# A planner's waiting times behind transfers, and the queue that stores projected values

## The chip, the cores and the metric

The kernel runs on one core of a Trainium2 chip. The metric is the time on the device in microseconds (us). Before the change it is 1178.59 us, the median of three runs (1177.14 to 1179.32).

## The reference

Four layers run in turn on one sequence of 2048 tokens with 640 channels: a sliding-window attention, a channel MLP, and both again with the same weights. Each adds to the residual `x`.

```python
# A: layernorm, then attention with W=8 keys at distance 2, 32 heads of 20 channels
qkv = x @ wqkv                                   # 640 -> 1920
idx = pos[:, None] - arange(8)[None, :] * 2      # each token looks at 8 earlier ones, two apart
attn = softmax(where(idx >= 0, q . k[idx] * 20**-0.5, -1e9))
x = x + (attn . v[idx]).reshape(S, 640) @ wo
# B: layernorm twice (once outside, once inside), then
x = x + gelu(y @ w1 + b1) @ w2 + b2              # 640 -> 1536 -> 640
# A, B, A, B
```

All arrays are float32.

## The kernel before, in words

**Tiles.** Tokens are split by parity (the window steps by two) and then into halves. That makes four units of 512 tokens, each 4 tiles of 128. With two layers of attention there are eight unit steps, numbered 0 to 7 (4 to 7 are the second layer). A unit's attention is done in four groups of eight heads, so there are 32 groups. The MLP of a unit walks through 12 blocks of 128 hidden channels; unit 0's MLP is done in two halves of 256 tokens.

**Precision.** Every float32 operand of a product is split into two fp16 parts, high and low, and three of the four partial products are taken. The split costs ScalarE (ACT) one copy and VectorE (DVE) one subtraction for each operand.

**One unit's way.** Layernorm (ACT, L524 to L560) gives `y`. It is split (L566 on ACT, L568 on DVE) and turned by four DMA transposes that SyncE's queue issues (L570). TensorE (PE) multiplies it by `wqkv`, 15 matmuls for each token tile and head group (L602). ACT copies each result from PSUM to `ev` (L617). Two token tiles of one head group make one `ev` buffer, of which there are three, and a DMA that ACT issues stores it to memory in `spill` (L623, called a put here; 64 of them). SyncE's queue fetches it back with a halo of neighbouring tokens into the single `qk` and the single `v` buffer (L642). DVE does the attention of a group there: products with q (L684), sums (L688), softmax (L693 to L703), products with v (L710), sums over the window (L718, L722). The result is split again (L729, L732) and turned by four DMA transposes (L745); PE multiplies it by `wo` (L756), and DVE adds the product to `x` (L762). A second layernorm and a third set of transposes follow (L570 again), and then the MLP: L810 is the first product, L816 the gelu, L819 and L821 its split, L831 the second product into five PSUM accumulators, L866 the addition to `x`. The MLP's weights are split once (L425, L426), stored by ACT's queue as `mw`, and loaded again for every unit by SyncE's queue (L803), into three buffers for each of the two matrices. The first product of the MLP waits for the split of all weights.

**What sets the order.** Nothing is scheduled by hand. Each step is handed to the class `Plan` as an operation: its engine, an estimated duration, a priority, what it needs, what it gives, and the buffers that it uses. `Plan.run` plays them in its own clock: of the operations that are ready it takes the earliest, and of equals the one with the lower priority. Then the instructions are emitted in the order of the planned start times, so each engine's queue has a fixed order. On the chip an engine that reaches an instruction early waits for it, and everything behind it on that engine waits too. So the planner's estimates set only the order.

**A transfer in the plan.** When an operation with `move` is placed, it joins its queue `REACH` later (L243), is drained there packet by packet (`SHARE` makes packets slower while two queues are busy), and counts as landed `LAND` later (L164). An operation that needs it may start `LAG["sp"]`, 0.05, after that (L182). A transpose occupies SyncE's queue for 1.45 in the plan (L378).

Of the kernel before, what the change touches and what calls it, by code (L numbers as in the profile page):

```python
# [20 lines left out]
GC = D // NG  # L21
# [43 lines left out]
class Plan:  # L65
# [9 lines left out]


    AHEAD = 3.0
    REACH = 0.45
    LAND = 1.4

    SHARE = 1.15

    LETS = ("pv", "hlo", "lo", "at", "xb")

# [24 lines left out]
    def run(self):  # L109
# [16 lines left out]
        soon, queues, late = [], {}, []  # L126
        seen = 0.0

        def done(o, end, lag):
            for u in o["use"]:  # L130
                self.users[u] -= 1
                self.last[u] = max(self.last.get(u, 0.0), end + lag * (u[0] != "pr" or o["eng"] != "dve"))
                if not self.users[u]:
                    self.free[u[0]].append((self.last[u], self.slot[u]))
            for k in o["give"]:
                when[k] = (o["eng"], end, bool(o["move"]))
                for w in waiting.pop(k, ()):
                    left[w["n"]] -= 1
                    if not left[w["n"]]:
                        ready.setdefault(w["eng"], []).append(w)  # L140
# [14 lines left out]
        def advance(t):  # L155
            h = heads()
            if h:
                turns = (t - seen) / turn()
                for x in h:
                    x[0] -= turns  # L160
            for x in h:
                if x[0] < 1e-9:
                    queues[x[2]["eng"]].pop(0)
                    late.append((t + self.LAND, x[2]))  # L164
            for b, o in [v for v in soon if v[0] <= t]:
                soon.remove((b, o))
                queues.setdefault(o["eng"], []).append([*o["move"], o])
            for e, o in [v for v in late if v[0] <= t]:
                late.remove((e, o))
                done(o, e, self.LAG["sp"])  # L170
            return t

        def start(o):
            t = clock[o["eng"]]
            if o["lazy"]:
                t = max(t, seen - self.AHEAD + sum(x[0] * x[1] for q in queues.values() for x in q)
                        + sum(v["move"][0] * v["move"][1] for _, v in soon))
            if o["pair"] and o["eng"] == "dve":
                t = max(t, port)
            for k in o["need"]:  # L180
                e, w, moved = when[k]
                w = w + (self.LAG["sp"] if moved else self.LAG[e] if e != o["eng"] else 0.06 * (e != "pe"))  # L182
                t = max(t, w)
            if o["pair"] and o["eng"] == "pool":
                for i, (a, b) in enumerate(reversed(shut)):
                    if t >= b:
                        break
                    if a <= t:
                        t = b + 0.1 * (i == 0)
                        break  # L190
            new = {}
            for u in o["use"]:
                if u in self.slot:
                    t = max(t, self.since[u])
                else:
                    fs = self.free[u[0]]
                    if u[0] in self.ORDERED and self.line[u[0]][self.turn.get(u[0], 0)] != u:
                        return None
                    i = new.get(u[0], 0)
                    if i >= len(fs):  # L200
                        return None
                    t = max(t, sorted(fs)[i][0])
                    new[u[0]] = i + 1
            return t

        total = len(self.ops)
        while len(order) < total:
            best = None
            for e, ops in ready.items():
                pick = None  # L210
                for o in ops:
                    t = start(o)
                    if t is None:
                        continue
                    key = (max(t - o["wait"], clock[e] + 0.05), o["prio"], o["n"])
                    if pick is None or key < pick[0]:
                        pick = (key, t, o)
                if pick and (best is None or (pick[1], pick[0]) < (best[1], best[0])):
                    best = pick
            then = event()  # L220
            if best is None and then == math.inf:
                raise RuntimeError(f"the plan is stuck: {[u for u in self.slot if self.users[u]]}")
            if best is None or then <= best[1]:
                seen = advance(then)
                continue
            _, t, o = best
            e = o["eng"]
            ready[e].remove(o)
            d = o["dur"]
            if o["table"] and o["table"] != table:  # L230
                table = o["table"]
                d += self.SWITCH
            for u in o["use"]:
                if u not in self.slot:
                    fs = self.free[u[0]]
                    fs.sort()
                    self.turn[u[0]] = self.turn.get(u[0], 0) + 1
                    self.since[u], self.slot[u] = fs.pop(0)
            o["at"] = t
            order.append(o)  # L240
            clock[e] = t + d
            if o["move"]:
                soon.append((t + self.REACH + 0.2 * (o["dur"] > 1), o))  # L243
                continue
            if e == "dve":
                kind = o["give"][0][0]
                if o["pair"]:
                    if shut and t - shut[-1][1] < 0.05 and before != "pv" and kind not in self.LETS:
                        shut[-1][1] = t + d
                    else:  # L250
                        shut.append([t, t + d])
                before = kind
            elif e == "pool" and o["pair"] and d > 1:
                port = t + d
            done(o, t + d, self.LAG[e])
# [6 lines left out]
def packet_time(n):  # L262
    return 0.0075 + n / 26.9e3
# [11 lines left out]
def sliding_dilated_then_mlp_kernel(  # L275
# [99 lines left out]
        plan.add(by, 0.1 if by == "act" else 0.38, prio, emit, need, give, use, move=(kb * 1e3 / 16 / packet, packet_time(packet)), lazy=lazy)  # L375

    def dma_transpose(prio, emit, need=(), give=(), use=()):
        plan.add("sp", 1.45, prio, emit, need, give, use, move=(80, packet_time(256) + 0.0045))  # L378

    def mm(cols, n, prio, emit, need=(), give=(), use=()):  # L380
        plan.add("pe", cols / 2400.0 + 0.0028 * n, prio, emit, need, give, use)
# [203 lines left out]
    def qkv(n):  # L585
# [6 lines left out]
        for k, (g, b) in enumerate(halves):  # L592
# [27 lines left out]

            def put(g=g, b=b, ek=ek):
                to = spill[la][par]
                nc.scalar.dma_start(  # L623
                    bass.AP(tensor=to.tensor, offset=to.offset + (g * 3 * ROWS + HALO + start + 2 * b) * GC,
                            ap=[[M * GC, P], [ROWS * GC, 3], [1, 2 * GC]]),
                    tile_of(*ek).rearrange("p a t c -> p a (t c)"))

            dma(P * 6 * GC * 4 / 1e3, -310 + n, put, need=[("ev", n, 2 * b + i, g) for i in range(2)],
                give=[("put", n, g, b)], use=[ek], by="act", packet=8 * GC)

    def fetch(G):
        n, g = divmod(G, NG)
# [319 lines left out]
```

## Time and profile before

| | |
|---|---|
| median of the runs | 1178.59 us (1177.14 to 1179.32) |
| the profiled execution's own time | 1177.89 us |
| its span, from the first instruction to the last | 1176.0 us |
| TensorE's granted clock over the span | 0.998 of full speed |
| busy: PE, DVE, ACT, POOL | 1157.5, 991.6, 511.5, 150.9 us |

The span is 1.9 us shorter than the execution's time. Busy time is the time in which an engine had at least one instruction in work. In rows of instructions the columns are start and duration in us, engine, line, operation, output<-input, shapes and count, and in square brackets the idle time of the engine just before and what ended it. `SPq` and `ACTq` are DMA issues on SyncE's and ACT's queue. In rows of waits the columns are who waited for whom, the sum in us, how often, and the longest.

### The profile page before, as it was taken

What the parts mean: (1) busy time and instruction counts of PE and PEld (TensorE: products, weight loads), DVE (VectorE), ACT (ScalarE), POOL (GpSimd) and SP (SyncE); (2) the same over time, 40 slices, a digit from 0 to 9 for tenths busy, and PEclk for the clock granted to TensorE, in tenths of its full rate; (3) what the DMA queues carried; (4) which work ended last, traced back from release to release, by engine and by line L of the source; (5) the groups of instructions that cost most, each with busy time, mean ns of one, the idle gap of its engine ahead of it and who ended that gap; (6) DMA issues with size and microseconds to landing.
All of it is one profiled execution on the core that took longest, in us unless ns stands there. A gap on an engine that the chain in (4) does not pass through costs nothing.

```text
span 1176.0 us, 17291 instructions
## 1 busy us (share of the span) xinstructions
PE 1157.5 (98%) x6902; PEld 626.5 (53%) x6902; DVE 991.6 (84%) x939; ACT 511.5 (43%) x925; POOL 150.9 (13%) x96
## 2 busy tenths in 40 slices
PE   8999999999999999999999999999999999999998
PEld 5444445577554455545554555555456555555554
DVE  7899999999899999999999999999999996311211
ACT  5485334436445345732537352376235423512121
POOL 1020102023011201320221012002120100000000
PEclk9999999999999999999999999999999999999999
DMA  9999997787776477567755865576555845633432
GB/s 294 300 329 283 373 349 195 212 269 243 210 205 196 162 215 188 176 191 190 193 180 177 212 167 188 202 166 186 188 177 161 246 158 128 154 103 102 145 101 79
DMA packets 219773, 235.01 MB, mean 200 GB/s; under 512 B 129884, under 2 KB 170412, under 8 KB 219692
## 3 DMA queue, kind: packets, MB, share of 16 engines
q1 hardware_dynamic: 190636, 194.57, 56.7%
q10 hardware_dynamic: 29056, 39.33, 9.6%
q8 instruction: 54, 0.88, 0.3%
q14 instruction: 27, 0.22, 0.1%
HBM read 158.93 MB, written 44.78 MB: 173 GB/s over the span
## 4 chain that ended last, share of the span: by engine, by line
PE 55%; DVE 28%; DMA 6%; issue 6%; ACT 4%; SPq 1%; POOL 0%; ACTq 0%; DVEq 0%; POOLq 0%
PE ps L602 20%; PE acc L831 14%; PE ps L810 14%; PE ps L756 7%; DVE pr L684 6%; DVE pr L710 6%; DVE pr L718 4%; DVE sm L688 4%; DMA yT<-w 2%; DVE act L821 1%; DMA qk<-spill 1%; ACT junk L528 1%; DMA act<-in_B_w_dram 1%; DVE w L722 1%; ACT junk L524 1%
## 5 line engine op out<-in xcount | busy, mean ns | idle before, releaser
L602 PE MATMUL ps<-wq,yT 128*128 128x480 f16 x1920 | 393.0, 367 | 4.8 <-DMA yT<-w 3.6
L831 PE MATMUL acc<-c,act 128*128 128x512 f16 (+1 forms) x2310 | 331.3, 299 | 1.1 <-DVE act L821 0.6
L810 PE MATMUL ps<-yT,c 128*128 128x512 f16 (+1 forms) x1620 | 328.6, 355 | 0.8 <-DMA c<-mw 0.8
L602 PEld LDWEIGHTS <-yT 128*128 128x128 f16 x1920 | 187.7, 98 | 207.0 <-DMA yT<-w 5.1
L831 PEld LDWEIGHTS <-act 128*128 128x128 f16 x2310 | 181.7, 98 | 143.3 <-DVE act L821 1.2
L810 PEld LDWEIGHTS <-c 128*128 128x128 f16 x1620 | 154.5, 98 | 147.1 <-DMA c<-mw 1.2
L816 ACT ACTIVATE act<-ps,b 128x512 f32<-128x512 f32 (+1 forms) x108 | 68.7, 637 | 272.4 <-PE ps L810 268.0
L684 DVE TENSOR_TENSOR pr<-qk 128x2560 f32<-128x2560 f32 x64 | 181.5, 2836 | 4.1 <-DMA qk<-spill 4.1
L710 DVE TENSOR_TENSOR pr<-sm,v 128x2560 f32<-128x2560 f32 x64 | 179.7, 2819 | 0.2
L688 DVE TENSOR_REDUCE sm<-pr 128x128 f32<-128x2560 f32 x64 | 179.5, 2805 | 0.1
L821 DVE TENSOR_TENSOR act<-act 128x512 f16<-128x512 f32 (+1 forms) x108 | 72.3, 671 | 124.1 <-ACT act L819 123.8
L718 DVE TENSOR_TENSOR pr<-pr 128x1280 f32<-128x1280 f32 (+1 forms) x128 | 144.8, 1151 | 0.2
L756 PE MATMUL ps<-wo,yT 128*128 128x320 f16 x960 | 132.4, 299 | 5.9 <-DMA yT<-ohl 3.3
L617 ACT ACTIVATE ev<-ps 128x480 f32<-128x480 f32 x128 | 71.6, 563 | 148.8 <-PE ps L602 137.3
L756 PEld LDWEIGHTS <-yT 128*128 128x128 f16 x960 | 93.7, 98 | 44.4 <-DMA yT<-ohl 4.3
L732 POOL TENSOR_TENSOR ohl<-w,ohl 128x640 f16<-128x640 f32 x24 | 67.1, 2796 | 379.2 <-ACT ohl L729 379.2
L541 POOL TENSOR_TENSOR ln<-ln,half 128x2 f32<-128x2 f32 (+1 forms) x30 | 36.2, 1207 | 451.0 <-ACT ln L538 451.0
L524 ACT ACTIVATE junk<-xf 128x640 f16<-128x640 f32 x56 | 41.1, 734 | 79.2 <-DVE xf L762 60.3
L819 ACT ACTIVATE act<-act 128x512 f16<-128x512 f32 (+1 forms) x108 | 62.4, 580 | 2.6
L568 DVE TENSOR_TENSOR w<-w,w 128x640 f16<-128x640 f32 x60 | 51.2, 874 | 1.5 <-ACT w L566 1.5
L560 ACT ACTIVATE w<-xf,ln 128x640 f32<-128x640 f32 x56 | 49.7, 908 | 1.9 <-DVE w L568 1.6
L566 ACT ACTIVATE w<-w 128x640 f16<-128x640 f32 x60 | 42.7, 727 | 12.5 <-DVE w L568 7.2
(53 smaller groups left out, 515.1 us busy)
## 6 DMA issues: line engine op xcount, KB each, us to landing
c<-mw SPq DMA_DIRECT2D x216, 320.0 KB, 3.2
spill<-ev ACTq DMA_DIRECT2D x64, 480.0 KB, 4.3
qk<-spill SPq DMA_DIRECT2D x32, 880.0 KB, 5.5
v<-spill SPq DMA_DIRECT2D x32, 880.0 KB, 4.5
qk<-spill SPq DMA_DIRECT2D x32, 320.0 KB, 3.2
act<-in_B_w_dram SPq DMA_DIRECT2D x24, 320.0 KB, 5.9
mw<-c ACTq DMA_DIRECT2D x24, 320.0 KB, 5.8
xf<-in_A_x_dram SPq DMA_DIRECT2D x16, 320.0 KB, 6.3
```

The lines of the kernel that those rows point to most:

```text
L602: nc.tensor.matmul(ps, transposed(yk)[:, a * KD + k, t * P:(t + 1) * P], wq[:, b, k, g], start=first and j == 0, stop=last and j == len(to ...
L617: act(3 * GC, -400 + n, lambda i=i, pk=pk, ek=ek: nc.scalar.activation(tile_of(*ek)[:, :, i], tile_of(*pk)[:, :3 * GC].rearrange("p (a c) ...
L684: nc.vector.tensor_mul(tile_of(*pk), w[:, HALO + m + t0:HALO + m + t0 + EH, None, :].to_broadcast([P, EH, W, GC]), windows(w, t0, [GC, W], ...
L688: dve(E, G - 0.7, lambda pk=pk, t0=t0: nc.vector.tensor_reduce(lg(t0, t0 + EH).rearrange("p t w h -> p (t w h)"), tile_of(*pk).rearrange(" ...
L710: nc.vector.tensor_mul(tile_of(*vk).rearrange("p t w (h d) -> p t (w h) d", d=DH), lg(t0, t0 + EH).rearrange("p t w h -> p t (w h)")[:, :, ...
L718: dve(EH * w * GC, G - 0.9, lambda vk=vk, w=w: nc.vector.tensor_add(tile_of(*vk)[:, :, 0:w], tile_of(*vk)[:, :, 0:w], tile_of(*vk)[:, :, w ...
L732: eng.tensor_sub(tile_of(*hk)[:, :, 1, g * GC:(g + 1) * GC], ot(), hi())
L756: nc.tensor.matmul(tile_of(*pk)[:, :D // 2], transposed(yk)[:, a * KD + k, t * P:(t + 1) * P], wo[:, b, k, c * D // 2:(c + 1) * D // 2], s ...
L810: nc.tensor.matmul(tile_of(*pk)[:, :nt], tile_of(*ck)[:, a, k * P:(k + 1) * P], transposed(yk)[:, c * KD + k, t0 * P:t1 * P], start=i == 0 ...
L816: act(nt, -430, lambda pk=pk, h32=h32, e=e: nc.scalar.activation(tile_of(*h32)[:, :nt], tile_of(*pk)[:, :nt], AF.Gelu_apprx_tanh, bias=b1[ ...
L821: dve(nt, -1000, lambda h32=h32, hk=hk: nc.vector.tensor_sub(tile_of(*hk)[:, 1, :nt], tile_of(*h32)[:, :nt], tile_of(*hk)[:, 0, :nt]), nee ...
L831: nc.tensor.matmul(accs[k][:, c0:c0 + n], tile_of(*hk)[:, a, (i - t0) * P:(i - t0 + 1) * P], tile_of(*wk)[:, c, w0:w0 + n], start=first, s ...
```

## The change

In the plan a transfer now joins its queue 0.75 after it is placed, or after its own duration where that is longer, pays 0.2 more at the head of the queue, and lands 0.9 later (0.5 for a transpose). Who needs the data waits a further time that depends on the engine: 2.0 for TensorE, 0.7 for ACT, DVE and POOL, none for SyncE. A transfer gives its buffers back 0.7 after it lands instead of 0.05. A transpose occupies the queue for 1.75. `SHARE` goes from 1.15 to 1.08. The puts are issued by SyncE's queue instead of ACT's, and so are planned on it. No operation is added or taken away.

```diff
     AHEAD = 3.0
-    REACH = 0.45
-    LAND = 1.4
-
-    SHARE = 1.15
+    REACH = 0.75
+    LAND = 0.9
+    RAMP = 0.2
+
+    SPARE = {"pe": 2.0, "act": 0.7, "dve": 0.7, "pool": 0.7, "sp": 0.0}
+
+    SHARE = 1.08
...
-                    late.append((t + self.LAND, x[2]))
+                    late.append((t + self.LAND - 0.4 * (x[2]["dur"] > 1), x[2]))
...
-                queues.setdefault(o["eng"], []).append([*o["move"], o])
+                queues.setdefault(o["eng"], []).append([o["move"][0] + self.RAMP / o["move"][1], o["move"][1], o])
...
-                done(o, e, self.LAG["sp"])
+                done(o, e, 0.7)
...
-                w = w + (self.LAG["sp"] if moved else self.LAG[e] if e != o["eng"] else 0.06 * (e != "pe"))
+                w = w + (self.LAG["sp"] + self.SPARE[o["eng"]] if moved else self.LAG[e] if e != o["eng"] else 0.06 * (e != "pe"))
...
-                soon.append((t + self.REACH + 0.2 * (o["dur"] > 1), o))
+                soon.append((t + max(self.REACH, o["dur"]), o))
...
     def dma_transpose(prio, emit, need=(), give=(), use=()):
-        plan.add("sp", 1.45, prio, emit, need, give, use, move=(80, packet_time(256) + 0.0045))
+        plan.add("sp", 1.75, prio, emit, need, give, use, move=(80, packet_time(256) + 0.0045))
...
             def put(g=g, b=b, ek=ek):
                 to = spill[la][par]
-                nc.scalar.dma_start(
+                nc.sync.dma_start(
...
-                give=[("put", n, g, b)], use=[ek], by="act", packet=8 * GC)
+                give=[("put", n, g, b)], use=[ek], packet=8 * GC)
```

Every engine's order changes. Three places follow; line numbers after the change are three higher in this part of the kernel.

**PE, where unit 5's attention result meets `wo`.** L756 (L759 after) is the product with `wo`, L831 (L834) the MLP's second product, L810 (L813) its first. Before:

```order
L831 MATMUL acc_100<-c_83,act 128x512
L831 LDWEIGHTS act
L831 MATMUL acc_101<-c_83,act 128x128
L756 LDWEIGHTS yT_72
L756 MATMUL ps_95<-wo,yT_72 128x320
```

After:

```order
L834 MATMUL acc_100<-c_83,act 128x512
L834 LDWEIGHTS act
L834 MATMUL acc_101<-c_83,act 128x128
L813 LDWEIGHTS c_80
L813 MATMUL ps_95<-yT_73,c_80 128x512
...
L759 LDWEIGHTS yT_72
L759 MATMUL ps_96<-wo,yT_72 128x320
```

The first product of one more hidden block, 15 matmuls of 512 columns, now stands ahead of the product with `wo`. The same count for the other places where PE takes up transposed data, as the number of matmuls by which the step comes later in PE's order (minus: earlier): `wo` of units 0 to 7: -30, +18, 0, +18, +18, +15, 0, +21; `wqkv` of unit 4's first half -27 and of its second half -62, of units 5, 6 and 7 +33, +18 and +15; unit 1's MLP +24.

**DVE, where unit 4's first layernorm result is split for its transposes.** L568 (L571) is that split, L710 (L713) the products with v of group 7, L718 and L722 (L721, L725) their sums, L821 (L824) the gelu's split. Before:

```order
L710 TENSOR_TENSOR pr_77<-sm_90,v_68 128x2560
L821 TENSOR_TENSOR act<-act 128x256
L718 TENSOR_TENSOR pr_77<-pr_77 128x2x640
L821 TENSOR_TENSOR act<-act 128x256
L718 TENSOR_TENSOR pr_77<-pr_77 128x2x320
L722 TENSOR_TENSOR w_84<-pr_77 128x320
L710 TENSOR_TENSOR pr_76<-sm_90,v_68 128x2560
L821 TENSOR_TENSOR act<-act 128x256
L568 TENSOR_TENSOR w_86<-w_88,w_86 128x640
```

After:

```order
L713 TENSOR_TENSOR pr_77<-sm_90,v_68 128x2560
L824 TENSOR_TENSOR act<-act 128x256
L571 TENSOR_TENSOR w_84<-w_88,w_84 128x640
L721 TENSOR_TENSOR pr_77<-pr_77 128x2x640
L824 TENSOR_TENSOR act<-act 128x256
L571 TENSOR_TENSOR w_85<-w_86,w_85 128x640
```

The split for the first transpose moves ahead of the sums of the group's first half and of the products of its second half. Elsewhere on DVE: unit 1's last split for its MLP comes six operations later (one L684, two L688 and three softmax steps are now ahead of it), unit 4's third split ten operations earlier, unit 5's first four later, unit 6's first is unmoved, and the last operation on unit 6's attention result comes one L701 later. The split of the last MLP weight block moves from DVE's 149th to its 182nd operation.

**SyncE's queue at the start.** L421 (L424) loads `x`, L414 (L417) clears the halo, L438 (L441) loads `wqkv`, L626 is the put. Before:

```order
L438 DMA pr_77<-in_A_wqkv_dram 128x5x160 x3
L438 DMA qk_67<-in_A_wqkv_dram 128x5x160 x3
L421 DMA xf<-in_A_x_dram 128x640 x4
L414 DMA spill_136<-act 7x12x160
...
L402 DMA b_104<-in_B_b_dram 128x12x1
```

After:

```order
L441 DMA qk_67<-in_A_wqkv_dram 128x5x160 x3
L626 DMA spill_135<-ev_69 128x3x320
L424 DMA xf<-in_A_x_dram 128x640 x4
L417 DMA spill_136<-act 7x12x160
...
L405 DMA b_104<-in_B_b_dram 128x12x1
L626 DMA spill_135<-ev_70 128x3x320
```

The put, which waits for a result of PE and ACT, now stands ahead of the loads of unit 1's `x`; further on, puts stand between the loads of the weights in the same way. Puts also stand directly ahead of the transposes of units 3's and 4's attention results (L748).

## The prediction

> **What bounds the kernel now.** I read the page's busy times first, then PE's waits, then the busy times by stretches, and last the timeline at each wait.
>
> ```profile
> span 1176.0 us, 17291 instructions
> PE 1157.5 (98%) x6902; PEld 626.5 (53%) x6902; DVE 991.6 (84%) x939; ACT 511.5 (43%) x925; POOL 150.9 (13%) x96
> PE 55%; DVE 28%; DMA 6%; issue 6%; ACT 4%; SPq 1%; POOL 0%; ACTq 0%; DVEq 0%; POOLq 0%
> ```
>
> PE is idle for 1176.0 - 1157.5 = 18.5 us, and the change takes no work from it: 18.5 us is the most that an order could give. The chain that ended last still runs through DVE for 28%. The stretches say why:
>
> ```profile
> 800.00:884.00 84.00, 84.00 (x458) 42.25 (x457) 83.06 (x71) 34.21 (x57) 19.10 (x9) 1.00 0.55 178
> 990.00:1176.00 186.00, 182.20 (x1135) 97.16 (x1132) 38.47 (x59) 46.82 (x80) 1.39 (x2) 1.00 0.41 117
> ```
>
> The columns after the stretch are its length and the busy time of PE, PEld, DVE, ACT and POOL, then clock, DMA share and GB/s. From 800 to 884 both PE and DVE are busy nearly all the time, and so they are before; only from 990 is PE alone. So a wait of PE that goes shortens the kernel only if DVE can hand over earlier as well. What PE waits for:
>
> ```profile
> PE ps L602 <- DMA yT<-w: 3.6, 3, 2.0
> PE ps L756 <- DMA yT<-ohl: 3.3, 2, 2.5
> PE ps L756 <- DVE xf L762: 2.6, 3, 0.9
> PE ps L810 <- DMA c<-mw: 0.8, 1, 0.8
> ```
>
> 7.7 us is spent on transfers, 6.9 of it on transposes. That is what spare time behind transfers can reach.
>
> **The change part by part.** *Unit 4's first transpose.*
>
> ```profile
> 286.83 2.82 DVE L710 TENSOR_TENSOR pr<-sm,v 128x2560 f32<-128x2560 f32 x1
> 289.64 1.80 PE L810 MATMUL ps<-yT,c 128*128 128x256 f16 x15
> 289.90 1.55 DVE L568 TENSOR_TENSOR w<-w,w 128x640 f16<-128x640 f32 x2
> 291.28 1.79 PE L831 MATMUL acc<-c,act 128*128 128x512 f16 x12
> 291.70 2.35 DVE L718 TENSOR_TENSOR pr<-pr 128x1280 f32<-128x1280 f32 x2
> 292.91 1.80 PE L810 MATMUL ps<-yT,c 128*128 128x256 f16 x15
> 296.68 3.58 PE L602 MATMUL ps<-wq,yT 128*128 128x480 f16 x10 [1.97 <-DMA yT<-w]
> 295.00:300.00 5.00, 3.32 (x10) 1.33 (x11) 4.62 (x4) 1.12 (x3) 0.00 (x0) 0.73 1.14 326
> 300.00:305.00 5.00, 5.00 (x26) 2.46 (x25) 3.46 (x4) 0.92 (x2) 0.00 (x0) 0.92 1.26 205
> 785.00:790.00 5.00, 2.56 (x19) 1.87 (x20) 2.73 (x4) 1.37 (x2) 0.00 (x0) 1.00 1.23 185
> ```
>
> The split (L568) moves ahead of one L710 (2.82), a pair of sums like L718's 2.35, and about 0.9 of smaller steps: 6.0 us earlier on DVE. PE reaches the product 27 matmuls earlier, a group of 15 and one of 12; such groups start 1.63 us apart (289.64, 291.28, 292.91), so 3.3 us. Net 2.7, more than the 1.97 waited. I expect DVE about 1.3 us late here (below) and leave 0.5 of the wait: gain 1.5. Behind this wait the clock was 0.73 and 0.92 of full for 5 us each, so (0.27 + 0.08) x 5 = 1.75 us were lost, which go with it. The wait of 2.47 us in 785 to 790 cost no clock (1.00), so this term can as well stay or appear elsewhere; it is 1.75 or nothing at each wait of about 2 us. [...]
>
> *Units 5 and 6, and unit 2's attention.* Of the 3.6 us under L602, 1.6 belong to units 5 and 6. Their products move back by 33 and 18 matmuls. At 3.24 us for 15 of the MLP's first product and 3.26 for 24 of its second (rows below) that is 3.24 + 18 x 0.136 = 5.7 and 18 x 0.136 = 2.5 us. DVE's split moves back by 4.2 (an L688 and three small steps) and 0: net 1.5 and 2.5, enough for both: gain 1.6. Unit 2's product with `wo` waits 3.3 - 2.47 = 0.8 and moves on neither engine: gain 0.4, between 0 and 0.8.
>
> *Unit 5's attention.*
>
> ```profile
> 778.03 0.80 SPq L642 DMA_DIRECT2D qk<-spill  x2
> 779.41 9.84 SPq L745 DMA_TRANSPOSE yT<-ohl  x4
> 787.44 2.75 PE L756 MATMUL ps<-wo,yT 128*128 128x320 f16 x19 [2.47 <-DMA yT<-ohl]
> 852.52 3.24 PE ps L810 x15
> 855.75 3.26 PE acc L831 x24
> ```
>
> The transposes stand behind a fetch on SyncE's queue that waits for DVE. That order stays. PE now does 15 more matmuls first, 3.24 us, against 2.47: gain 2.47. The one MLP load that PE waited for (0.8) has 12 more matmuls, 1.6 us, ahead of its user: gain 0.8. The 2.6 us of waits for L762 are no transfers: 0, at most 2.6.
>
> *New waits.*
>
> ```profile
> 334.62 6.22 SPq L570 DMA_TRANSPOSE yT<-w x2
> 347.14 3.40 PE L810 MATMUL ps<-yT,c 128*128 128x512 f16 x15
> 376.12 2.91 SPq L570 DMA_TRANSPOSE yT<-w  x2
> 379.60 5.63 PE L602 MATMUL ps<-wq,yT 128*128 128x480 f16 x27
> yT<-w SPq DMA_TRANSPOSE x60, 4.4
> ```
>
> Unit 1's MLP had its last transpose issued near 338, 9 us ahead. DVE now does six more operations before it, 9.9 us (one L684 of 2.8, two L688 of 2.8, the rest softmax), and PE 24 more matmuls, 3.3 us; that leaves about 3 where a landing takes 4.4. Unit 4's second half had 379.60 - 376.12 = 3.5 us and keeps 3.1, since PE comes 62 matmuls earlier (2 x 3.24 + 32 x 0.136 = 10.8 us) and DVE ten operations (10.4 us). Together I charge 2.5 us, between 0 and 5.
>
> *The puts.*
>
> ```profile
> L623 ACTq DMA_DIRECT2D spill<-ev x64: 366/367/1044, 20.1 to 853.2; - x64
> SPq L803 <- PE acc L831: 197.2, 84, 16.0
> ```
>
> 64 x 0.37 = 23.5 us of issuing leaves ACT (43% busy) and lands on SyncE's queue, which waits 197 us for MLP buffers alone and so has room. Behind a waiting put stand fetches, transposes and loads. No row shows a put on that queue; ahead of units 3's and 4's transposes it costs at most 480 KB at 326 GB/s, 1.5 us, covered by the 18 matmuls (2.5 us) that those products move back. I take 0.
>
> *Weights.*
>
> ```profile
> 169.30 0.82 DVE L426 SCALAR_TENSOR_TENSOR c<-act,c 128x640 f16<-128x640 f32 x1
> 225.62 5.08 PE L810 MATMUL ps<-yT,c 128*128 128x256 f16 x45
> ```
>
> 33 operations of attention, 39 us, now stand ahead of the last weight split: 170 + 39 = 209 against PE's first MLP product at 225.6. The cover is 17 us; I take 0.
>
> Sum for PE: 1.5 + 1.75 + 1.6 + 0.4 + 2.47 + 0.8 - 2.5 = 6.0 us.
>
> *What DVE allows.* Unit 6's product with `wo` is at the same row of PE's order as before, and its last DVE operation is one L701 (0.6 us) later.
>
> ```profile
> 883.94 5.97 SPq L745 DMA_TRANSPOSE yT<-ohl  x4
> 888.08 6.28 PE L756 MATMUL ps<-wo,yT 128*128 128x320 f16 x45
> yT<-ohl SPq DMA_TRANSPOSE x32, 3.8
> DVE xf L762 <- PE ps L756: 19.8, 15, 3.1
> DVE pr L684 <- DMA qk<-spill: 4.1, 6, 1.3
> ```
>
> 883.94 + 3.8 = 887.7: PE started 0.3 us after the landing. Whatever PE gained before, it can be here only as much earlier as DVE. DVE's own waits: 4.1 us for fetches, of which I let 3 go, since a fetch's user now has 0.7 more in the plan; about 9.8 of the 19.8 for L762 lie before 884 (the rest after 990), and 6 of them are behind the two late `wo` products of units 1 and 5, which I let go. Against that DVE is held by unit 0's product with `wo` and by late ACT results between 190 and 270; I charge 3. DVE comes 3 + 6 - 3 - 0.6 = 5.4 us earlier. The smaller of 6.0 and 5.4 counts, since PE works without a gap from there: gain 5.4.
>
> 1177.9 - 5.4 = 1172.5 for the profiled execution, which was 0.7 under the median of the runs; on the scale of the median 1173.
>
> **Rivals.** *DVE gives nothing back (no change).* If DVE's waits only change their places, the product at 888.08 starts when it did and PE's gains are spent there waiting. The same row in both orders and 98.9% (83.06 of 84.00) of DVE's time speak for it; that the largest of DVE's waits hang on PE's own late products speaks against. It gives 1178.6.
>
> *DVE is late (slower).* The weight splits now run at 170 to 209 us between attention and the residuals of unit 0, each behind its load (5.9 us to land), which stands behind a put that waits for PE.
>
> ```profile
> act<-in_B_w_dram SPq DMA_DIRECT2D x24, 320.0 KB, 5.9
> DVE c L426 <- ACT c L425: 2.1, 4, 0.8
> ```
>
> Four such waits cost 2.1 us before. If the last twelve pieces wait 0.8 us each, DVE loses 9.6 there, against the 9 that it gains: with the 3.6 charged above it is 9.6 + 3.6 - 9 = 4.2 us late at 884, and so is the end: 1182.8. It decides once these waits pass 9 - 3.6 = 5.4 us. Against it: between load and split stand 9 to 14 us in the new orders, more than 5.9 and ACT's copy.
>
> *All waits go.* PE's 7.7, the clock's 1.75 and the 2.6 for L762 make 12, DVE's 4.1 and 9.8 allow it: 1166.5.
>
> **How the numbers follow.** The forecast, some part of the waits gone, has 0.62; all gone 0.05; no change 0.18; slower 0.15. A run of this kernel can tell 0.2% (2.4 us) from no change. Faster than 1176.2: 0.67; within: 0.18; slower than 1181: 0.15. The bounds of my terms (new waits 0 to 5, L762 0 to 2.6, unit 2 0 to 0.8, the clock) reach from 1167 to 1177, and the case of no change takes the range up to 1181.
>
> **What would show it.** Right: the waits under L602 and L756 for transposes fall from 6.9 us to 3 or less, none at 296 and 787; the clock stays at 1.00 from 295 to 305; PE's idle time falls to about 13; unit 6's `wo` starts at about 882.5. Wrong: `wo` of unit 6 at 888 with a wait of several us in front (first rival); the last L429 after 215 us with waits for ACT's L428 (second); a wait of 2 us or more near 350 or 370 with the clock at half behind it.

## The result, and the profile after

The changed kernel takes 1171.45 us (median of 4 runs, 1170.73 to 1171.96) beside 1178.95 for the kernel before on the same chip: a ratio of 0.9933, 95% interval 0.9910 to 0.9956. Measured once more among the experiments it gave 0.9923 (0.9910 to 0.9936). In medians that is 7.5 us less, and 8.9 the second time (1178.98 to 1170.13); the forecast of 1173.0 was 5.6 under the 1178.59 of before. The profiled execution took 1170.73 us.

First the page of the kernel after: the span, the busy times, and the shares of the chain that ended last.

```profile
span 1168.9 us, 17323 instructions
PE 1153.9 (99%) x6902; PEld 625.5 (54%) x6902; DVE 993.6 (85%) x939; ACT 508.8 (44%) x923; POOL 157.5 (13%) x96
PE 63%; DVE 7%; ACT 2%; issue 2%; DMA 2%; POOL 0%; SPq 0%; DVEq 0%
```

PE is idle for 1168.9 - 1153.9 = 15.0 us instead of 18.5 (about 13 were forecast), and its busy time is 3.6 us shorter with the same 6902 matmuls. DVE's share of the chain falls from 28% to 7%. Next the rows of PE's waits that the text uses, then DVE's waits of the two kinds that the prediction counted:

```profile
PE ps L759 <- DMA yT<-ohl: 3.5, 3, 1.6
PE ps L605 <- ACT wq L428: 2.6, 1, 2.6
...
PE acc L834 <- ACT act L822: 0.9, 1, 0.9
PE acc L834 <- DVE act L824: 0.8, 1, 0.8
...
PE ps L759 <- DVE xf L765: 0.5, 1, 0.5
```

```profile
DVE xf L765 <- PE ps L759: 12.9, 13, 1.5
DVE pr L687 <- DMA qk<-spill: 2.2, 2, 1.7
```

The transposes' waits fall from 6.9 us to 3.5, and those under `wqkv` (L602 before) are gone. So is the wait for a weight load. L762's waits (2.6) are down to 0.5. What is new stands at the kernel's start: 2.6 us for ACT's split of `wqkv`. Three signs that the prediction named were met only in part: it wanted 3 us or less for transposes, none at 787 (0.68 us are left, at 784.31 below), and about 13 us of idle time. The stretches that the prediction named, with the columns as there:

```profile
295.00:300.00 5.00, 5.00 (x27) 2.43 (x25) 4.97 (x6) 1.74 (x4) 0.00 (x0) 1.00 0.74 257
300.00:305.00 5.00, 5.00 (x27) 2.38 (x26) 4.38 (x5) 2.26 (x4) 0.00 (x0) 1.00 1.08 277
785.00:790.00 5.00, 5.00 (x39) 3.62 (x37) 5.00 (x6) 1.35 (x3) 0.00 (x0) 1.00 1.11 211
```

All three are full, and the clock stays at 1.00 where it was at 0.73 and 0.92. Last the steps themselves, from the timeline of PE and of SyncE's queue:

```profile
290.61 1.58 PE L605 MATMUL ps<-wq,yT 128*128 128x480 f16 x7
307.20 3.03 PE L759 MATMUL ps<-wo,yT 128*128 128x320 f16 x21 [1.24 <-DMA yT<-ohl]
348.14 2.10 PE L813 MATMUL ps<-yT,c 128*128 128x512 f16 x9
366.52 1.78 PE L605 MATMUL ps<-wq,yT 128*128 128x480 f16 x8
422.85 2.35 PE L759 MATMUL ps<-wo,yT 128*128 128x320 f16 x16 [1.55 <-DMA yT<-ohl]
784.31 5.88 PE L759 MATMUL ps<-wo,yT 128*128 128x320 f16 x42 [0.68 <-DMA yT<-ohl]
876.74 5.95 SPq L748 DMA_TRANSPOSE yT<-ohl  x4
881.70 2.47 PE L759 MATMUL ps<-wo,yT 128*128 128x320 f16 x17
```

Unit 4's `wqkv` (290.61), unit 1's MLP (348.14) and unit 4's second half (366.52) wait for nothing. Unit 6's `wo` starts at 881.70 instead of 888.08, where 882.5 was named. Its transposes are issued 7.2 us earlier (876.74 against 883.94), and the first of them lands at 880.15, 1.5 us ahead of PE; before it landed at 887.35, 0.7 ahead. Up to there PE won 6.4 us, and by the end 7.1.

### The profile page after: what moved, and what is told of

It is laid out like the page before. It is cut to its first block, busy times and chain, and to the rows that moved or that the text cites. A ratio compares the mean times of both kernels' runs of the same rounds, so it can differ in the third digit from the quotient of the medians.

```text
span 1168.9 us, 17323 instructions
## 1 busy us (share of the span) xinstructions
PE 1153.9 (99%) x6902; PEld 625.5 (54%) x6902; DVE 993.6 (85%) x939; ACT 508.8 (44%) x923; POOL 157.5 (13%) x96
## 4 chain that ended last, share of the span: by engine, by line
PE 63%; DVE 7%; ACT 2%; issue 2%; DMA 2%; POOL 0%; SPq 0%; DVEq 0%
PE acc L834 21%; PE ps L813 20%; PE ps L605 13%; PE ps L759 9%; DVE pr L687 2%; DVE pr L713 2%; DVE pr L721 1%; DMA yT<-ohl 1%; DVE sm L691 1%; DMA qk<-spill 1%; ACT junk L531 0%; ACT act L819 0%; DVE w L571 0%; ACT L702 0%; DVE act L824 0%
## 5 line engine op out<-in xcount | busy, mean ns | idle before, releaser
L834 PE MATMUL acc<-c,act 128*128 128x512 f16 (+1 forms) x2310 | 330.6, 299 | 2.2 <-ACT act L822 0.9
L813 PE MATMUL ps<-yT,c 128*128 128x512 f16 (+1 forms) x1620 | 328.2, 355 | 0.0
L834 PEld LDWEIGHTS <-act 128*128 128x128 f16 x2310 | 181.6, 98 | 144.0 <-ACT act L822 1.1
L813 PEld LDWEIGHTS <-c 128*128 128x128 f16 x1620 | 154.6, 98 | 146.4
L713 DVE TENSOR_TENSOR pr<-sm,v 128x2560 f32<-128x2560 f32 x64 | 179.4, 2818 | 0.2
L824 DVE TENSOR_TENSOR act<-act 128x512 f16<-128x512 f32 (+1 forms) x108 | 70.7, 656 | 124.4 <-ACT act L822 124.1
L721 DVE TENSOR_TENSOR pr<-pr 128x1280 f32<-128x1280 f32 (+1 forms) x128 | 144.5, 1150 | 0.1
L759 PE MATMUL ps<-wo,yT 128*128 128x320 f16 x960 | 132.0, 299 | 3.9 <-DMA yT<-ohl 3.5
L735 POOL TENSOR_TENSOR ohl<-w,ohl 128x640 f16<-128x640 f32 x24 | 70.5, 2939 | 422.3 <-ACT ohl L732 413.2
L759 PEld LDWEIGHTS <-yT 128*128 128x128 f16 x960 | 93.7, 98 | 42.6 <-DMA yT<-ohl 4.9
L822 ACT ACTIVATE act<-act 128x512 f16<-128x512 f32 (+1 forms) x108 | 62.5, 580 | 2.7
L571 DVE TENSOR_TENSOR w<-w,w 128x640 f16<-128x640 f32 x60 | 49.5, 839 | 5.2 <-ACT w L569 5.2
L732 ACT ACTIVATE ohl<-w 128x640 f16<-128x640 f32 x32 | 23.4, 733 | 55.9 <-DVE w L725 55.8
```

Of the source, the lines that this page charges most:

```text
L713: nc.vector.tensor_mul(tile_of(*vk).rearrange("p t w (h d) -> p t (w h) d", d=DH), lg(t0, t0 + EH).rearrange("p t w h -> p t (w h)")[:, :, ...
L721: dve(EH * w * GC, G - 0.9, lambda vk=vk, w=w: nc.vector.tensor_add(tile_of(*vk)[:, :, 0:w], tile_of(*vk)[:, :, 0:w], tile_of(*vk)[:, :, w ...
L735: eng.tensor_sub(tile_of(*hk)[:, :, 1, g * GC:(g + 1) * GC], ot(), hi())
L759: nc.tensor.matmul(tile_of(*pk)[:, :D // 2], transposed(yk)[:, a * KD + k, t * P:(t + 1) * P], wo[:, b, k, c * D // 2:(c + 1) * D // 2], s ...
L813: nc.tensor.matmul(tile_of(*pk)[:, :nt], tile_of(*ck)[:, a, k * P:(k + 1) * P], transposed(yk)[:, c * KD + k, t0 * P:t1 * P], start=i == 0 ...
L824: dve(nt, -1000, lambda h32=h32, hk=hk: nc.vector.tensor_sub(tile_of(*hk)[:, 1, :nt], tile_of(*h32)[:, :nt], tile_of(*hk)[:, 0, :nt]), nee ...
```

## The experiments

The prediction says that the rows of the new order carry the gain: waits for transposes that go, the clock behind one of them, and a hand-over from DVE that comes earlier. Against it stand theories by the parts of the edit: that spare time alone (theory 1 where the expectations number them), the puts on SyncE's queue alone (theory 2), or the new times alone (theory 3) make the gain. There are three parts with two settings each, so eight kernels, of which before and after are two. The table has all runs. PE's waits are summed over the profiled execution, with gaps under 0.15 us and without the 1.35 us ahead of its first matmul. The clock lost is half of the time at half clock, from the first rise of the clock on: the one stretch of the kernel before is 3.41 us long (297.34 to 300.75) and cost 1.7 us, and the other figures of the column, up to 8.5, are multiples of 1.7. Where PE waits inside a stretch the column counts too much. The remainder is the span less both: PE's own work, with the span's start and end. The profile is of a single execution, which can lie far from the median: those of spare time alone and of spare time for PE alone are of their slowest, 4.5 and 5.0 us above it. (before's median is 1178.6 to 1179.0 in the measurements beside the kernels.)

| kernel | ratio to before (95% interval) | median us | profiled span | PE's waits | clock lost | remainder |
|---|---|---|---|---|---|---|
| before | 1 | 1178.7 | 1176.0 | 13.8 | 1.7 | 1160.5 |
| spare time alone | 0.9974 (0.9955 to 0.9993) | 1176.81 | 1179.5 | 16.0 | 5.1 | 1158.4 |
| new times alone | 1.0044 (1.0029 to 1.0058) | 1184.53 | 1182.8 | 18.6 | 6.8 | 1157.4 |
| puts alone | 1.0020 (1.0010 to 1.0030) | 1180.86 | 1177.4 | 14.1 | 3.4 | 1159.9 |
| spare time and new times | 0.9991 (0.9983 to 1.0000) | 1178.71 | 1176.8 | 12.4 | 5.1 | 1159.3 |
| spare time and puts | 1.0032 (1.0020 to 1.0044) | 1182.58 | 1180.2 | 19.3 | 1.7 | 1159.2 |
| new times and puts | 0.9974 (0.9962 to 0.9987) | 1175.56 | 1174.6 | 13.6 | 1.7 | 1159.3 |
| all three (after, again) | 0.9923 (0.9910 to 0.9936) | 1170.13 | 1168.7 | 9.5 | 0 | 1159.2 |
| after's order, ACT issues the puts | 0.9954 (0.9938 to 0.9969) | 1172.75 | 1170.4 | 12.0 | 0 | 1158.4 |
| after's order, 6.5 us more on DVE | 0.9953 (0.9940 to 0.9965) | 1174.36 | 1170.8 | 11.3 | 0 | 1159.5 |
| after's order, 6.5 us less on DVE | 0.9911 (0.9895 to 0.9927) | 1168.62 | 1171.0 | 9.0 | 3.4 | 1158.6 |
| after, spare time for PE alone | 1.0098 (1.0080 to 1.0116) | 1190.17 | 1193.4 | 25.4 | 8.5 | 1159.5 |
| after, PE's spare time 3.0 | 1.0034 (1.0022 to 1.0046) | 1182.84 | 1181.6 | 18.8 | 5.1 | 1157.7 |

### One part at a time

*Spare time alone.* The kernel before, with

```diff
+    SPARE = {"pe": 2.0, "act": 0.7, "dve": 0.7, "pool": 0.7, "sp": 0.0}
...
-                w = w + (self.LAG["sp"] if moved else self.LAG[e] if e != o["eng"] else 0.06 * (e != "pe"))
+                w = w + (self.LAG["sp"] + self.SPARE[o["eng"]] if moved else self.LAG[e] if e != o["eng"] else 0.06 * (e != "pe"))
```

> The kernel before with SPARE alone added; old landing and transpose times, puts by ACT. Theory 1: 1170 to 1174, transposes waited for 4 us or less. Theories 2 and 3: 1177 to 1181.

0.9974, a third of the gain: 1176.81 lies beside the forecasts of all three theories, just under that of theories 2 and 3. Its twelve runs spread from 1169.5 to 1181.3. PE's waits in its profile, of the slowest:

```profile
PE acc L833 <- ACT act L821: 4.6, 1, 4.6
PE ps L604 <- DMA yT<-w: 4.2, 3, 2.2
```

The transposes under `wqkv` still cost 4.2 us in spite of the spare time, and the MLP's start costs 4.6.

*The puts alone.* The kernel before, with the puts on SyncE's queue:

```diff
-                nc.scalar.dma_start(
+                nc.sync.dma_start(
...
-                give=[("put", n, g, b)], use=[ek], by="act", packet=8 * GC)
+                give=[("put", n, g, b)], use=[ek], packet=8 * GC)
```

> The kernel before with the puts planned on and issued by SyncE's queue, nothing else. Theory 1 and theory 3: 1176 to 1181, no change. Theory 2: 1171 to 1174.

1.0020 (1.0010 to 1.0030): slower by 0.2%, inside the range that theories 1 and 3 forecast. The waits under L602 are 4.0 us where before had 3.6.

*The new times alone.* The kernel after, with

```diff
-    SPARE = {"pe": 2.0, "act": 0.7, "dve": 0.7, "pool": 0.7, "sp": 0.0}
+    SPARE = {"pe": 0.0, "act": 0.0, "dve": 0.0, "pool": 0.0, "sp": 0.0}
...
-                nc.sync.dma_start(
+                nc.scalar.dma_start(
...
-                give=[("put", n, g, b)], use=[ek], packet=8 * GC)
+                give=[("put", n, g, b)], use=[ek], by="act", packet=8 * GC)
```

> The changed kernel without spare time and with the puts by ACT: only the new landing and transpose times stay. Theory 3 (these times make the better order): 1173 to 1176, as without spare time. If the half of the gain that stayed there belongs to the puts: 1178 to 1180.

1.0044, slower, and outside both forecasts. PE's longest waits, the last split of a weight on DVE with the loads that follow on SyncE's queue, and the stretches around the wait:

```profile
PE ps L813 <- DMA c<-mw: 7.0, 3, 6.5
PE ps L605 <- DMA yT<-w: 4.4, 3, 2.4
```

```profile
221.61 0.82 DVE L429 SCALAR_TENSOR_TENSOR c<-act,c 128x640 f16<-128x640 f32 x1
227.00 3.76 SPq L806 DMA_DIRECT2D c<-mw  x6
```

```profile
225.00:230.00 5.00, 1.25 (x12) 0.88 (x9) 5.00 (x6) 2.39 (x4) 0.00 (x0) 0.85 0.92 304
230.00:235.00 5.00, 2.30 (x11) 1.64 (x12) 5.00 (x4) 0.74 (x1) 0.78 (x1) 0.50 1.00 370
```

In this order the last weight is split at 221.6, and the loads of the split weights go out at 227: 6.5 us of waiting, and 10.2 us of half clock that begin inside it. PE stands idle for 4.2 of these, so they cost 3.0 us and not the 5.1 that the table counts. This is what the second rival foresaw (the last L429 after 215), though by the split's place in the order and not by its waits; the kernel after splits its last weight by 209.7.

### Two parts at a time

*Spare time and new times* is the kernel after with the two put lines as they were before.

> The changed kernel with the puts planned on and issued by ACT's queue as before; spare time, landing and transpose times stay. Theory 1 (spare time and new times make the order, the queue is neutral): 1170 to 1174, not to be told from the changed kernel. Theory 2 (the puts on SyncE's queue are worth something once the other two are there): 1175 or more.

0.9991, almost nothing: theory 2's side of the forecast (1175 or more), and theory 1 has failed. *New times and puts* is the kernel after with the `SPARE` line all 0.0.

> The changed kernel with all five entries of SPARE at 0; the new landing times, the longer transposes and the puts on SyncE's queue stay. Theory 1 (spare time): the waits of TensorE for transposes come back to 6 us or more and the time to 1177 to 1181. Theory 2 (puts) and theory 3 (the new landing and transpose times make the better order): 1170 to 1173, and TensorE's waits for transposes stay near 3.5 us.

0.9974, between the two forecasts. The waits for transposes are back at 6.7 us, as theory 1 said, but the time isn't at its 1177 to 1181. *Spare time and puts* is the first kernel of these with the puts of the second.

> The spare time and the puts on SyncE's queue, with the old times for landing and transposes: the last of the eight combinations of three parts. Theory that the parts add up: spare time alone gave 0.9974 and the puts alone 1.002, so 0.9994, about 1178 us. Theory that every combination is another order, whose time is about 1159 us of span plus TensorE's waits plus the clock lost behind them: the product of two ratios says nothing; the time follows the waits of its own profile, a span of 1159 + waits + 1.7 for each half-clock window to within 1 us, and can lie anywhere from 1170 to 1182 us. Theory that it is spare time with puts on SyncE's queue that makes the gain, and the new times nothing: 1170 to 1172 us.

1.0032: slower than before, where the sum of its two parts would be 0.9994. The span is 1159 + 19.3 + 1.7 = 1180.0 by the second theory, and 1180.2 measured. The waits are no longer at the transposes alone:

```profile
PE ps L758 <- DVE xf L764: 3.9, 3, 1.8
PE acc L833 <- DMA c<-mw: 2.5, 1, 2.5
```

*All three*, as a control:

> The changed kernel once more, beside the others of this set: 1170 to 1174, ratio 0.992 to 0.996.

0.9923, and 0 of clock lost.

What follows from the eight: no part has an effect of its own that holds from one order to the next. The puts change the ratio by +0.20% when added to before, +0.58% when added to spare time, -0.70% when added to the new times and -0.68% when added to both. Spare time changes it by -0.26% alone, +0.12% with the puts, -0.53% with the new times and -0.51% with both. The new times change it by +0.44% alone, +0.17% with spare time, -0.46% with the puts and -1.09% with both. The steps of 0.12 and 0.17% are too small for the intervals; the others have both signs for each part. All three theories by parts fall. The remainder in the table lies between 1157.4 and 1160.5 in all thirteen profiles. That PE's work is constant is no surprise, since no operation was added for it; what it says is that of the difference of up to 24 us all but about 3 lies in PE's waits and the clock behind them, and the rows show these at places that differ from order to order. Part of the 3 us is clock too: PE starts at half of its later rate (its matmuls of 128 columns start 107 ns apart up to 7.21 us in before and up to 5.26 in after, and 56 ns apart from there on), and the table counts waiting inside a half-clock stretch twice. PE's busy time less half of what it worked at half clock, the start included, is 1152.9 us in before and 1151.9 in after.

### The order after, and close to it

*The order kept, the puts issued by ACT.* Only the call is changed, not the plan:

```diff
-                nc.sync.dma_start(
+                nc.scalar.dma_start(
```

> The order of the changed kernel, but ACT issues the 64 puts again at the same places of the order (the plan still counts them on SyncE's queue). Theory 1 (the gain is the order that the spare time makes; the issuing queue costs and gives nothing): 1171.5 within 1.5 us, ratio to the kernel before 0.993 to 0.994. Theory 2 (the gain is that ACT and its waits are rid of the puts): most of the 7.5 us is lost, 1176 to 1179, and the waits of ACT's evictions for put landings come back.

0.9954, so most of the gain is the order's and not the queue's. The rest shows in single runs, each of which has its mean clock on record. Of 11 runs, the five with a clock of 1.00 average 1170.5 us, as the kernel after does (1170.3 in the four of its second measurement, all at 1.00; the first had two at 1.00 and two at 0.998, 1170.7 to 1172.0, with no difference between them); the six at 0.997 to 0.999 average 1175.0. The profile, of a run at 1.00, has a wait of 2.56 us at 307.2 where the kernel after has 1.24, and one of 2.28 at 313.7 where it has none:

```profile
PE ps L759 <- DMA yT<-ohl: 7.2, 4, 2.6
```

```profile
305.00:310.00 5.00, 2.80 (x21) 2.05 (x22) 4.04 (x3) 0.25 (x1) 0.00 (x0) 1.00 1.11 159
310.00:315.00 5.00, 2.72 (x21) 1.74 (x20) 5.00 (x4) 0.00 (x0) 0.00 (x0) 1.00 1.25 266
```

Two waits of over 2 us, and no clock lost in this run. That in the six others the clock was lost behind these same waits is likely and not shown, since only one run has a trace, and the mean clock also counts the time behind PE's last matmul (in the kernel before that ends at 1172.72 us, and the clock is at half from 1174.56 on).

*DVE with more work.* The causal mask is added twice, 16 operations of 0.41 us more:

```diff
-            dve(L, G - 0.8, lambda: nc.vector.tensor_add(
-                lg(), lg(), mask[:, :, :, None].to_broadcast([P, m, W, GH])), need=[*last, "mask"], give=[("lm", G)], use=[sk])
+            def masked():
+                for _ in range(2):
+                    nc.vector.tensor_add(lg(), lg(), mask[:, :, :, None].to_broadcast([P, m, W, GH]))
+
+            dve(L, G - 0.8, masked, need=[*last, "mask"], give=[("lm", G)], use=[sk])
```

> The changed kernel's order with the mask added twice in the 16 groups that have it: 16 more operations of 0.41 us on DVE, 6.5 us in all before unit 6's attention ends. (The mask is doubled, which leaves masked weights at zero.) Handover theory (DVE and PE are both full until 880 us, so what DVE is late PE is late): 3 to 6 us slower than the changed kernel, with TensorE waiting longer for the transposes of L745's kind. Rival (PE is the bound and DVE has room): under 1 us.

1174.36, or 4.2 us over the kernel after, as the handover theory forecast. But the waits for transposes, 3.8 us in all, did not grow (3.5 and 4.1 in the two profiles of the kernel after): unit 2's `wo` waits 2.44 instead of 1.55 and 1.93, unit 1's less. A wait of 1.0 for a weight load is new, and those for the residual (L768 here) are 0.9 where they were 0.5 and 0.3. Two of its six runs had a clock of 1.00 and average 1171.8, 1.5 us over the kernel after; the four others average 1174.8. How much of the 4.2 is clock stays open.

*DVE with less work.* The same with `range(0)`, which leaves the mask out.

> The order of the kernel after, word for word, but without the addition of the causal mask (16 operations of VectorE of 0.41 us, 6.5 us in all, most of them before 884 us); the first tokens' attention is thereby computed without the mask. If VectorE still sets part of TensorE's hand-overs, 1 to 4 us faster than the kernel after (at most the 5.6 us of waits that TensorE has there between 228 and 790 us). If VectorE no longer sets the time, no change (within 1 us). With the mask twice it was 4.2 us slower.

1168.62, 1.5 us under the kernel after and inside its interval, so by itself not a proof. The three runs at a clock of 1.00 average 1168.0, that is 2.3 us under. The profile is of its slowest run: unit 1's transposes came 3.03 us late there (L762 here is the product with `wo`), and 6.8 us of half clock came with it.

```profile
PE ps L762 <- DMA yT<-ohl: 4.2, 2, 3.0
```

```profile
305.00:310.00 5.00, 1.97 (x9) 0.90 (x8) 2.57 (x1) 0.57 (x1) 0.00 (x0) 0.77 0.75 156
310.00:315.00 5.00, 5.00 (x22) 2.92 (x21) 5.00 (x6) 0.00 (x0) 0.00 (x0) 0.55 1.04 288
```

Of 6.5 us on DVE, 1.5 to 2.3 reach the end in runs at full clock. So in the order after DVE probably still hands on some of its time, a quarter to a third, by waits that it lengthens; it isn't the bound. With two and three such runs, beside a kernel after whose six at 1.00 lie between 1169.3 and 1172.0, the share is an estimate.

### The numbers of the change varied

*Spare time for PE alone.*

```diff
-    SPARE = {"pe": 2.0, "act": 0.7, "dve": 0.7, "pool": 0.7, "sp": 0.0}
+    SPARE = {"pe": 2.0, "act": 0.0, "dve": 0.0, "pool": 0.0, "sp": 0.0}
```

> The kernel after, with spare time for TensorE alone (2.0) and none for ACT, DVE and POOL. If TensorE's spare time is the part that acts, 1170 to 1173 us, as the kernel after. If the 0.7 of the others is needed, because VectorE's waits for fetches come back and with them its late hand-overs, VectorE waits 2 us or more longer for its fetches than after (2.2 us there) and the time is 1174 to 1177 us. Every order being another, a wait of TensorE of over 2 us at another transpose would also make it 1174 or more, and then the fetch waits have not grown.

1190.17, 1.0098: far outside the forecast, though VectorE's waits for fetches did grow, from 2.2 to 5.8 us. They are too small for the 20 us. PE's waits show more (its profile is of the slowest run, 1195.2 us):

```profile
PE ps L759 <- DVE xf L765: 8.2, 5, 3.8
PE acc L834 <- DMA c<-mw: 4.2, 1, 4.2
PE acc L834 <- ACT act L822: 2.7, 1, 2.7
```

```profile
334.45 5.17 SPq L573 DMA_TRANSPOSE yT<-w  x2
339.72 0.61 SPq L626 DMA_DIRECT2D spill<-ev  x1
340.76 0.34 SPq L806 DMA_DIRECT2D c<-mw  x1
341.22 1.72 SPq L573 DMA_TRANSPOSE yT<-w  x1
343.04 1.38 SPq L645 DMA_DIRECT2D qk<-spill  x2
344.51 3.85 SPq L806 DMA_DIRECT2D c<-mw  x6
```

The second rows are SyncE's queue ahead of the 4.2 us (which PE waits at 347.5): the MLP's loads stand behind transposes, a put and a fetch, and six of them go out only at 344.51. In the kernel after the first four are there at 336.41:

```profile
336.41 3.89 SPq L806 DMA_DIRECT2D c<-mw  x4
```

*PE's spare time 3.0.*

```diff
-    SPARE = {"pe": 2.0, "act": 0.7, "dve": 0.7, "pool": 0.7, "sp": 0.0}
+    SPARE = {"pe": 3.0, "act": 0.7, "dve": 0.7, "pool": 0.7, "sp": 0.0}
```

> Spare time of 3.0 instead of 2.0 for TensorE, all else as after. If what is left of TensorE's waits for transposes (3.5 us) is spare time that was too short, they fall to about 1 us and the time to 1168 to 1170 us. If the waits left belong to the hand-over from VectorE, more spare time in the plan only moves them: 1170 to 1173. If the plan's order is spoilt elsewhere by the extra time (an MLP that is started too early waits for its split), slower than 1173.

1182.84, 1.0034: the third case. The waits for transposes do fall, to 0.8 us, and a single wait of another kind costs more than they all:

```profile
PE acc L834 <- ACT act L822: 7.5, 1, 7.5
PE ps L759 <- DVE xf L765: 3.9, 5, 2.1
PE ps L759 <- DMA yT<-ohl: 0.8, 1, 0.8
```

```profile
226.40 0.47 ACT L819 ACTIVATE act<-ps,b 128x256 f32<-128x256 f32 x1
232.56 0.74 ACT L732 ACTIVATE ohl<-w 128x640 f16<-128x640 f32 x1 [5.69 <-DVE w L725]
233.21 0.40 ACT L822 ACTIVATE act<-act 128x256 f16<-128x256 f32 x1
```

PE's second MLP product needs the split L822, which stands in ACT's order behind a copy (L732) that waits 5.69 us for DVE's attention. From inside it on the clock is at half for 10.2 us (0.88, 0.50 and 0.60 of full in the 5 us stretches from 225 to 240), of which PE stands idle for 4.9, so that 2.7 us are lost and not the 5.1 of the table. So spare time doesn't only move a product behind its transfer: it moves what is put in its place, and here that was an MLP block ahead of its cover.

## Why the prediction was right

**PE's sum.** By its terms, forecast and measured (in us, from the waits of both profiles): unit 4's first transpose 1.5, and 1.97; the clock behind it 1.75, and 1.71; units 5 and 6 1.6, and 1.6 (both waits gone); unit 5's `wo` 2.47, and 1.79 (0.68 is left); the MLP load 0.8, and 0.85. Unit 2's `wo` was to gain 0.4 and lost 0.72 (0.83 to 1.55). Five of the six came out, within 0.7, in these two profiles.

**New waits.** 2.5 us were charged at unit 1's MLP and unit 4's second half; both measured 0. The margins were too small: the prediction left about 3 us for unit 1 (its own terms make 9 - 9.9 + 3.3 = 2.4) and 3.1 for unit 4. The trace has 4.7 and 4.6. For unit 1:

```profile
343.47 1.41 SPq L573 DMA_TRANSPOSE yT<-w  x1
```

It is issued 5.7 us later than before (337.81) where DVE's operations made 9.9, and PE comes 1.0 later (348.14 against 347.14) where its matmuls made 3.3. So DVE had already won 4.2 us by there and PE 2.3. The step that failed is this margin, which left both out. It lands 4.2 us later, 0.5 ahead of PE. A new wait of 1.24 came where none was forecast: unit 1's product with `wo`.

**L762's waits.** Charged at 0 with 2.6 as the bound; they gave 2.1. All three old waits are gone, one of 0.48 is new. The mechanism was named, its size not taken.

**The start.** Not in the sum. PE's waits in the first 20 us grew from 2.41 to 3.95, but the steps are hardly later. PE's first product with `wqkv`, before, after, and in the second profile of the kernel after:

```profile
10.02 3.34 PE L602 MATMUL ps<-wq,yT 128*128 128x480 f16 x15 [1.15 <-ACT yT L487]
10.52 3.20 PE L605 MATMUL ps<-wq,yT 128*128 128x480 f16 x15 [2.57 <-ACT wq L428]
9.79 3.20 PE L605 MATMUL ps<-wq,yT 128*128 128x480 f16 x15 [1.62 <-ACT wq L428]
```

The clock rose at 7.21 us before and at 5.26 after, so PE arrived 0.9 us sooner and waited longer. The step is 0.5 us later in one profile of the kernel after and 0.2 earlier in the other, so no loss at the start is shown to be the order's.

Gains of 1.97 + 1.71 + 1.6 + 1.79 + 0.85 + 2.1 less 0.72, 1.24 and 1.54 make 6.5. Small waits at 228 to 232 and 278 for the MLP's split grew from 0.57 to 1.64, which leaves 5.4. That is also the difference of waits and lost clock of the two profiles, 13.8 + 1.7 - 10.1. The remainder fell by 1.8 us as well, all of it before 884. Of this 1.0 is that earlier rise of the clock, the other side of the waits at the start; the place of the other 0.8 stays open. That the forecast of the sum (6.0) and PE's 6.4 lie so close is partly luck: 2.5 us charged for nothing and 2.1 not taken stand against waits of about the same size that the prediction did not have.

**What DVE allows.** Forecast 5.4 us earlier at unit 6's transposes, measured 7.2 (883.94 to 876.74). The waits for fetches gave 1.9 of the 3 that were counted. Of those for L762 the prediction placed 9.8 us before 884; the trace has 7.3 there, and 2.8 after the change:

```profile
DVE xf L762 <- PE ps L756: 7.3, 7, 3.1
DVE xf L765 <- PE ps L759: 2.8, 6, 0.6
```

The waits behind the late `wo` products of units 1 and 5 are gone, 6.5 us where 6 were counted. Of the 3 us charged against that, 1.5 came at unit 0's product with `wo`. Elsewhere DVE stood idle for 3.5 us less, which no term had, and it worked 2.7 us longer where 0.6 was counted. So this total is close partly by luck as well. The step was sound, that DVE has to come earlier by as much; DVE's share of the chain, 28% before and 7% after, fits it. But which of the two counts would be the smaller came out the other way round: PE's 6.4 us ended last.

**The puts.** 0 was taken. In the same order the issuing queue makes no difference that shows in runs at full clock (1170.5 and 1170.3). Over all runs SyncE's queue is 0.2 to 0.3% faster, at the edge of what the intervals can tell apart. As a part of the plan the puts made from +0.58 to -0.70%, which is the order again.

**Weights.** The last weight split ends at 209.7, where 209 was worked out, and no wait comes of it:

```profile
207.41 2.28 DVE L429 SCALAR_TENSOR_TENSOR c<-act,c 128x640 f16<-128x640 f32 x3
```

**The rivals.** "DVE gives nothing back" falls with the 7.2 us. "DVE is late" falls for this order, since DVE's waits for ACT under L429 came to 4.1 us for the MLP's weights, none over 1.0, under the 5.4 at which it would have decided; it was no idle thought, since new times alone lost 6.5 us at that place. "All waits go" did not come: 3.5 us for transposes and 0.5 for L765 are left of 10.3.

**The clock.** The term of 1.75 us came as forecast in the two profiles. It does not make the gain of the medians: of 76 runs of the kernel before, the seven with a mean clock of 1.00 average 1178.3 us (1176.7 to 1180.6), and the six of the kernel after at 1.00 lie between 1169.3 and 1172.0. Why the wait of 1.97 us there cost clock and the one of 2.47 us in the same profile none is not shown.

That the direction was right has a likely reason: the prediction counted in the new order's rows, place by place, and did not argue from what spare time is for. The purpose alone would have forecast the same gain for PE's spare time at 3.0, which is slower than before.

## What to carry to other kernels

Here no number of the planner had an effect of its own: each setting makes another order, an engine that waits at one instruction holds up what stands behind it (with PE's spare time at 3.0 ACT's copy L732 waited 5.69 us, and the split L822 behind it with it), and this kernel's neighbours lie between 1170 and 1190 us without a trend. So read the order that comes out at every place where an engine takes up transferred data, count both engines' operations ahead of it, add what each engine has already won by there, and look at the kernel's start and at the first step of each new stage too; or try a number of settings and keep the best, knowing that the best is a find and not a rule. In this kernel the wait of PE of 1.97 us cost 1.7 us of clock more and the one of 2.47 us in the same profile nothing more, so an estimate should carry both prices for a wait of 2 to 2.6 us.

## What the runs showed of the hardware

In the profile of the kernel before, TensorE's clock is at half from 297.34 to 300.75 us, or for 3.41 us. PE works all that time, so 1.7 us are lost. The wait of 1.97 us that ended at 296.68 stands just ahead. That wait and others, with the mean clock of the 5 us stretches behind them:

| kernel | wait of PE, us | clock behind it | clock lost, us |
|---|---|---|---|
| before | 1.97 (to 296.68) | 0.73 and 0.92 from 295 to 305 | 1.7 |
| before | 2.47 (to 787.44) | 1.00 from 785 to 795 | 0 |
| after | 2.57 (to 10.52) | 1.00 up to PE's end | 0 |
| after's order, ACT issues the puts | 2.56 and 2.28 | 1.00 from 305 to 315 | 0 |
| after's order, 6.5 us more on DVE | 2.44 (to 423.71) | 1.00 from 420 to 430 | 0 |
| after's order, 6.5 us less on DVE | 3.0 | 0.77 and 0.55 from 305 to 315 | 3.4 |
| after, spare time for PE alone | 4.2 (at 347.5) | 0.66 from 350 to 355 | 1.7 |
| new times alone | 6.5 | 0.85, 0.50 and 0.63 from 225 to 240 | 5.1 |
| after, PE's spare time 3.0 | 7.55 (to 233.66) | 0.88, 0.50 and 0.60 from 225 to 240 | 5.1 |

In the last two part of the half clock falls into the wait itself, so only 3.0 and 2.7 us of the 5.1 are lost. Three more profiles have clock lost though no wait of PE in them is over 2.6 us: puts alone (longest wait 2.6, 3.4 lost), spare time and puts (2.5, 1.7) and new times and puts (2.3, 1.7). In the second profile of the kernel after the longest wait is 1.9, and 0 is lost.

So a wait of about 2 us cost 3.7 us in one place of the kernel before, and one of 2.47 us there cost 2.47. What decides between the two is not shown. That clock lost behind such waits makes the spread between runs of one kernel (1170.5 and 1175.0 with the puts issued by ACT, 1171.8 and 1174.8 with more work on DVE) is likely and not shown either; the runs of the kernel before have no such spread (1178.3 at 1.00, 1178.8 at 0.998).
